# Another order of the parts of a steady step in a fused attention and feed-forward kernel

## The chip, the cores and the metric

The kernel runs on one core of a Trainium2 chip. The core has five engines that work side by side, each with its own queue of instructions in a fixed order: TensorE (PE in the profile; its weight loads are the row PEld), VectorE (DVE), ScalarE (ACT), GpSimd (POOL) and SyncE (SP, which here only issues DMAs). An instruction starts when its engine has come to it and when what it waits for is done. The metric is the device time of one execution in microseconds (us).

## The reference, cut to what matters

```python
scores = q @ k.T / sqrt(64)                      # 4 batches, 8 heads, 768 positions, 64 wide
keep   = (key < n_sink) | (0 <= row - key < window)      # 4 sinks, window of 128
a      = softmax(where(keep, scores, -1e9))
x      = (a @ v)  -> rows of 8 * 64 = 512        # 3072 tokens
h      = x @ w_in                                # 512 -> 2048
g      = max(h, 0) + log1p(exp(-abs(h)))
out    = g @ w_out                               # 2048 -> 512
```

## The kernel before

The 3072 tokens are cut into 12 chunks of 256 (three chunks to a batch). The work is laid out in steps: step i is head i % 8 of chunk i // 8, and in one step every part of the pipeline does one unit of its own: attention for one head, and one eighth of the two dense layers of an earlier chunk. All engines run their instructions in the order in which the Python code emits them, so the order of the parts within a step is the order of each engine's queue. Steps 0 to 16 are a list written out by hand (`Ctx.START`), with the loading of the weights between; from step 17 on `_fast` runs the parts J, j, G, L and then the letters of `Ctx.STEADY`: its second string where i % 8 is 0 (called the switch step below, because there the first dense layer goes over to the next chunk), its first string in the seven others. A step later than the switch step is called step 1 of the chunk, and so on to step 7.

The letters, with the lines and the tile names that the profile shows:

- S `scores` of head i + 4: 4 matmuls into `s` (lines 230, 231). T `softmax` of the same head: DVE masks and reduces `s` (243, 249), ACT takes exponentials (250). N `normalise`: DVE `sm`, `rc` (256, 257), and POOL scales `a` (264).
- W `weights_t` of head i: 2 transposes into `t` (297), ACT copies to `th`, DVE makes the rest `tl`, POOL masks both into `pt` (4 selects, 308 and 311). V `values`: 3 to 4 matmuls into `x` (327, 333) that need `pt`. O `out`: ACT copies `xt`, DVE adds `xt` and `xf` (351, 352); after an odd head ACT makes `xh` and POOL `xl` (DVE after head 7).
- p `split` of head i + 5 (ACT `qkh`, DVE the rests `qkh` and `kl`), q `split_v` (ACT and POOL, `vv`, odd steps alone), k and K the sink columns (`sa`, `ts`, `sk`, each fourth step).
- U: one eighth of the first dense layer, 24 matmuls into `h` (459). F `softplus`: three passes on ACT (466 to 468) into `mt`. P `gate`: DVE adds (474), POOL rounds to `gh` (52). R `residue`: DVE `gl`, the rest of the eighth before. D and E: the two halves of the second dense layer, two eighths behind U, 6 matmuls each (496 to 498) that need `gh` and `gl`.
- J and j put the sink values `vs` of a new batch in place on POOL (lines 151, 152, 60, 159), heads 0 to 3 at the start of step 6 and heads 4 to 7 at the start of step 1; in the steady part this happens three times each, when a batch ends. A weight check on DVE (440) follows most even steps.

Every product is done in parts: high and low halves of each operand are multiplied apart and added in PSUM, which is why there are so many splits. `t` and `x` have one PSUM buffer each, `s` and `h` two.

Of the kernel before, what the change touches and what calls it, by code (L numbers as in the profile page):

```python
# [834 lines left out]
Ctx.WT = "PAAVVVVAVAAVAAAVAAAAAAAAAAAPAAAV"  # L835
Ctx.WH = "VAPAAVAAAAVPPAAAAVVAVAAAAAVAVAAA"
Ctx.WL = "PPPPPPPVPPVPPVPPVPVPPPPVVPVVPVPV"
Ctx.STEADY = ("kWRqpUKFSTDPNVOE", "kqWRpSDKTUFNPVEO")
Ctx.START = """
S0 G4 T0 w w S1 j4 T1 J0 w L8 w w S3 S2 N0 N1 T2 W0 L10 w N2 S4 T3 N3 a w T4 k0 a c K0 a S5 c W1 w w  # L840
d S6 V0 O0 l d V1 w c l T5 N4 W2 T6 d w a S7 c O1 W3 l N5 G6 N6 a T7 c V2 N7 a d S8 k4 a O2 W4 w T8
# [62 lines left out]
```

## Time and profile before

| | |
|---|---|
| median of 3 runs | 738.54 us (738.09 to 738.7) |
| the profiled execution | 735.03 us |
| its span, first to last instruction | 733.3 us |
| mean granted clock of TensorE | 0.987 |
| PE busy | 699.0 us, 95% |
| DVE, ACT, POOL busy | 567.5, 448.7, 429.0 us |

The steady steps run from about 120 us to the end of the span; an ordinary one takes 6.8 to 6.9 us. Start times in the rows are us from the first instruction of the profiled execution.

### The profile page before, as it was taken

What the parts mean: (1) busy time and instruction counts of PE and PEld (TensorE: products, weight loads), DVE (VectorE), ACT (ScalarE), POOL (GpSimd) and SP (SyncE); (2) the same over time, 40 slices, a digit from 0 to 9 for tenths busy, and PEclk for the clock granted to TensorE, in tenths of its full rate; (3) what the DMA queues carried; (4) which work ended last, traced back from release to release, by engine and by line L of the source; (5) the groups of instructions that cost most, each with busy time, mean ns of one, the idle gap of its engine ahead of it and who ended that gap; (6) DMA issues with size and microseconds to landing.
All of it is one profiled execution on the core that took longest, in us unless ns stands there. A gap on an engine that the chain in (4) does not pass through costs nothing.

```text
span 733.3 us, 13867 instructions
## 1 busy us (share of the span) xinstructions
PE 699.0 (95%) x4489; PEld 621.4 (85%) x4489; DVE 567.5 (77%) x1608; ACT 448.7 (61%) x1098; POOL 429.0 (59%) x773
## 2 busy tenths in 40 slices
PE   4788899999999999999999999999999999999996
PEld 3567688988999999888898999998898998998995
DVE  5899997887887887887987988888887887754331
ACT  3577865765666666765666765765666666644331
POOL 4866476675655765775765665666666576563110
PEclk9899999999999999999999999999999999999998
DMA  8877611411321321312222222221222222100001
GB/s 299 298 261 227 196 40 48 119 53 44 100 67 48 106 67 49 103 55 60 74 74 67 77 77 67 77 75 46 71 66 78 77 67 77 60 11 1 29 1 35
DMA packets 40876, 63.21 MB, mean 86 GB/s; under 512 B 4635, under 2 KB 22363, under 8 KB 40795
## 3 DMA queue, kind: packets, MB, share of 16 engines
q1 hardware_dynamic: 36042, 45.47, 21.4%
q10 hardware_dynamic: 4752, 16.77, 6.7%
q8 instruction: 38, 0.62, 0.4%
q14 instruction: 44, 0.35, 0.2%
HBM read 55.93 MB, written 6.29 MB: 85 GB/s over the span
## 4 chain that ended last, share of the span: by engine, by line
PE 80%; DVE 7%; ACT 5%; POOL 5%; issue 2%; DMA 1%; ACTq 0%; SPq 0%; POOLq 0%; DVEq 0%
PE h L459 33%; PE acc L496 10%; PE acc L498 10%; PE acc L497 10%; PE x L333 6%; PE t L297 2%; PE s L230 2%; PE s L231 2%; ACT a L250 2%; PE x L327 2%; PE s L227 1%; DVE wt L403 1%; ACT mt L467 1%; ACT mt L468 1%; POOL vs L159 1%
## 5 line engine op out<-in xcount | busy, mean ns | idle before, releaser
L459 PE MATMUL h<-xh,wi 128*128 128x256 f32 x1536 | 254.1, 288 | 0.0
L459 PEld LDWEIGHTS h<-xh,wi 128*128 128x128 f32 x1536 | 211.7, 192 | 1.3 <-issue 0.3
L52 POOL TENSOR_SCALAR gh<-mt 128x512 fp32r<-128x512 f32 x91 | 56.6, 622 | 169.4 <-DVE mt L474 164.3
L459 PE MATMUL h<-xl,wi 128*128 128x256 f32 x768 | 154.7, 283 | 0.0
L496 PE MATMUL acc<-wo,gh 128*128 128x512 f32 x384 | 152.3, 397 | 0.0
L498 PE MATMUL acc<-wo,gl 128*128 128x512 f32 x384 | 151.3, 394 | 0.8 <-DVE gl L56 0.8
L497 PE MATMUL acc<-wo,gh 128*128 128x512 f32 x384 | 151.1, 393 | 0.0
L474 DVE SCALAR_TENSOR_TENSOR mt<-h,mt 128x512 f32<-128x512 f32 x96 | 66.1, 689 | 73.0 <-ACT mt L468 63.9
L466 ACT ACTIVATE mt<-h 128x512 f32<-128x512 f32 x96 | 57.1, 595 | 102.6 <-PE h L459 102.1
L459 PEld LDWEIGHTS h<-xl,wi 128*128 128x128 f32 x768 | 119.8, 192 | 0.0
L250 ACT ACTIVATE a<-a,stats 128x136 f32<-128x136 f32 x192 | 76.1, 397 | 59.7 <-DVE stats L249 59.7
L264 POOL TENSOR_SCALAR a<-a,rc 128x128 f32<-128x128 f32 x180 | 68.1, 390 | 43.0 <-ACT mt L466 28.3
L498 PEld LDWEIGHTS acc<-wo,gl 128*128 128x128 f32 x384 | 72.4, 189 | 17.7 <-DVE gl L56 1.2
L496 PEld LDWEIGHTS acc<-wo,gh 128*128 128x128 f32 x384 | 72.4, 189 | 13.0 <-issue 0.5
L56 DVE TENSOR_TENSOR gl<-mt,gh 128x512 fp32r<-128x512 f32 x96 | 77.4, 806 | 4.1 <-POOL gh L52 4.0
L497 PEld LDWEIGHTS acc<-wo,gh 128*128 128x128 f32 x384 | 72.5, 189 | 8.9
L308 POOL TENSOR_SCALAR_AFFINE_SELECT pt<-tl 128x256 fp32r<-128x256 f32 x80 | 57.9, 724 | 17.6 <-DVE tl L56 17.6
L467 ACT ACTIVATE mt<-mt 128x512 f32<-128x512 f32 x96 | 60.8, 633 | 3.1
L468 ACT ACTIVATE mt<-mt 128x512 f32<-128x512 f32 x96 | 60.7, 632 | 3.1
L48 ACT CAST qkh<-qk 128x656 fp32r<-128x656 f32 x80 | 59.5, 744 | 2.4 <-DMA qk<-qk 2.3
L308 POOL TENSOR_SCALAR_AFFINE_SELECT pt<-th 128x256 fp32r<-128x256 f32 (+1 forms) x96 | 41.8, 435 | 27.5 <-ACT th L48 20.2
L56 DVE TENSOR_TENSOR kl<-qk,qkh 128x400 fp32r<-128x400 f32 x80 | 53.7, 671 | 2.5
(183 smaller groups left out, 1247.2 us busy)
## 6 DMA issues: line engine op xcount, KB each, us to landing
qk<-qk SPq DMA_DIRECT2D x160, 164.0 KB, 3.0
vr<-v SPq DMA_DIRECT2D x32, 192.0 KB, 2.8
out<-o SPq DMA_DIRECT2D x24, 256.0 KB, 2.3
q<-q SPq DMA_DIRECT2D x8, 256.0 KB, 4.9
vr<-v SPq DMA_DIRECT2D x16, 128.0 KB, 2.2
k<-k SPq DMA_DIRECT2D x8, 200.0 KB, 4.8
wi00r<-w ACTq DMA_DIRECT2D x1, 511.8 KB
wi01r<-w ACTq DMA_DIRECT2D x1, 511.8 KB
```

Of the source, the lines that this page charges most:

```text
L48: nc.scalar.copy(out, in_)
L56: (nc.vector if eng == "V" else nc.gpsimd).tensor_tensor(out, a, b, ALU.subtract)
L250: nc.scalar.activation(a, a, AF.Exp, bias=nm, scale=-1.0, accum_out=sm[:, j : j + 1])
L264: (nc.vector if eng == "V" else nc.gpsimd).tensor_scalar(a, a, rc[:, j : j + 1], 0.0, ALU.mult, ALU.add)
L308: nc.gpsimd.affine_select(pt[:, e, :, 1], src[:], [[0, CH], [1, P]], ALU.is_ge, 0.0, base=0, channel_multiplier=-1)
L459: nc.tensor.matmul(h[:, j], wt, x, start=k == 0, stop=k >= len(prods) - 2, skip_group_check=True)
L467: nc.scalar.activation(t[:], t[:], AF.Exp, scale=-1.0)
L468: nc.scalar.activation(t[:], t[:], AF.Ln, bias=1.0)
L474: nc.vector.scalar_tensor_tensor(t[:], h[:], 0.0, t[:], ALU.max, ALU.add)
L496: nc.tensor.matmul(acc[:], gh[:, j, q], wh, start=f == 0, stop=False, skip_group_check=True)
L497: nc.tensor.matmul(acc[:], gh[:, j, q], wl, start=False, stop=False, skip_group_check=True)
L498: nc.tensor.matmul(acc[:], gl[:, j, q], wh, start=False, stop=f == 2 * FP - 1, skip_group_check=True)
```

## The change

One line: the two strings that give the order of the parts of a step from step 17 on.

```diff
-Ctx.STEADY = ("kWRqpUKFSTDPNVOE", "kqWRpSDKTUFNPVEO")
+Ctx.STEADY = ("kWUqpKSFTRDVPONE", "SWTkpUKERDNFPqVO")
```

No instruction is added or removed. What moves on each engine:

TensorE. In the seven other steps its order stays as it was (W, U, K, S, D, V, E). In the switch step it changes. The rows are from the switch step into chunk 8, `t_0` the transposes of head 0, `s_4` the scores of head 4, `acc` the second dense layer, `ts` the sink transposes, `h_0` the first dense layer. Before:

```order
L297 MATMUL t_0_7077<-ident,a_0_6730 128x128 x2
L230 MATMUL s_4_0_7096<-qkh_4_6993 128x264
L231 MATMUL s_4_0_7096<-kl_4_6996,qkh_4_6993 128x264
L230 MATMUL s_4_1_7099<-qkh_4_6993 128x264
L231 MATMUL s_4_1_7099<-kl_4_6996,qkh_4_6993 128x264
L496 MATMUL acc_0_6534<-wo_1193,gh_6_6949 128x512
L497 MATMUL acc_0_6534<-wo_1193,gh_6_6949 128x512
L498 MATMUL acc_0_6534<-wo_1193,gl_6_6988 128x512
L496 MATMUL acc_1_6535<-wo_1193,gh_6_6949 128x512
L497 MATMUL acc_1_6535<-wo_1193,gh_6_6949 128x512
L498 MATMUL acc_1_6535<-wo_1193,gl_6_6988 128x512
L281 MATMUL ts_0_7108<-ident,sa_0_7075 32x128 x2
```

And in the changed kernel, at the same place:

```order
L230 MATMUL s_4_0_7075<-qkh_4_7016 128x264
L231 MATMUL s_4_0_7075<-kl_4_7019,qkh_4_7016 128x264
L230 MATMUL s_4_1_7078<-qkh_4_7016 128x264
L231 MATMUL s_4_1_7078<-kl_4_7019,qkh_4_7016 128x264
L297 MATMUL t_0_7081<-ident,a_0_6728 128x128 x2
L459 MATMUL h_0_7109<-xh_6356,wi_316 128x256 x4
L459 MATMUL h_0_7109<-xl_6357,wi_316 128x256 x2
L459 MATMUL h_0_7109<-xh_6356,wi_316 128x256 x4
L459 MATMUL h_0_7109<-xl_6357,wi_316 128x256 x2
L459 MATMUL h_0_7109<-xh_6356,wi_329 128x256 x4
L459 MATMUL h_0_7109<-xl_6357,wi_329 128x256 x2
```

The 24 matmuls of U have moved ahead of the six of D; behind them now come K, E, D and, last, V (before: V, then E).

VectorE. In the seven other steps `gl` goes from ahead of the split to behind T, and `sm` and `rc` go behind `xt` and `xf`. In the switch step, from `tl_0` on, before:

```order
L56 TENSOR_TENSOR tl_0_7082<-t_0_7077,th_0_7080 128x256
L56 TENSOR_TENSOR gl_7_7089<-mt_7_7023,gh_7_7047 128x512
L56 TENSOR_TENSOR qkh_5_7091<-qk_5_6973,qkh_5_7091 64x256
L56 TENSOR_TENSOR kl_5_7094<-qk_5_6973,qkh_5_7091 128x400
L56 TENSOR_TENSOR sk<-ts_0_7108,sk 32x256
L243 COPY_PREDICATED s_4_0_7096<-diag,s_4_0_7096 128x128
L243 COPY_PREDICATED s_4_1_7099<-diag,s_4_1_7099 128x128
L249 ISA a_1_7113,stats<-s_4_0_7096,mask_141 128x136
```

And now:

```order
L56 TENSOR_TENSOR tl_0_7086<-t_0_7081,th_0_7084 128x256
L243 COPY_PREDICATED s_4_0_7075<-diag,s_4_0_7075 128x128
L243 COPY_PREDICATED s_4_1_7078<-diag,s_4_1_7078 128x128
L249 ISA a_1_7093,stats<-s_4_0_7075,mask_141 128x136
L249 ISA stats 128x1
L249 ISA a_1_7093,stats<-s_4_1_7078,mask_142 128x136
L249 ISA stats 128x1
L269 TENSOR_TENSOR sa_0_7102<-a_0_6728,rc_0_6729 128x64
L56 TENSOR_TENSOR qkh_5_7104<-qk_5_6973,qkh_5_7104 64x256
L56 TENSOR_TENSOR kl_5_7107<-qk_5_6973,qkh_5_7104 128x400
L56 TENSOR_TENSOR sk<-ts_0_7134,sk 32x256
L56 TENSOR_TENSOR gl_7_7145<-mt_7_7027,gh_7_7052 128x512
```

T stands first now, and `gl` last. On ACT the exponentials of T go ahead of `qkh` in the same way.

GpSimd. After an odd head `xl` goes ahead of the two scalings of N. The rows are the end of a step 5 and the start of the step 6 behind it, where J puts sink values in place (`vsh` to the second `vs`). Before:

```order
L52 TENSOR_SCALAR gh_5_4427<-mt_5_4403 128x512
L264 TENSOR_SCALAR a_0_4313<-a_0_4313,rc_0_4314 128x128 x2
L56 TENSOR_TENSOR xl_3940<-xf_4_4340,xh_3939 128x256
L151 TENSOR_SCALAR vsh_4452<-vsr_4450 64x128
L152 TENSOR_TENSOR vsr_4450<-vsr_4450,vsh_4452 64x128
L60 TENSOR_SCALAR vs_0_4455<-sk 64x512
L159 TENSOR_TENSOR vs_0_4455<-vsh_4452,hmask 64x4x64
```

And now:

```order
L52 TENSOR_SCALAR gh_5_4432<-mt_5_4407 128x512
L56 TENSOR_TENSOR xl_3940<-xf_4_4336,xh_3939 128x256
L264 TENSOR_SCALAR a_0_4311<-a_0_4311,rc_0_4312 128x128 x2
L151 TENSOR_SCALAR vsh_4452<-vsr_4450 64x128
L152 TENSOR_TENSOR vsr_4450<-vsr_4450,vsh_4452 64x128
L60 TENSOR_SCALAR vs_0_4455<-sk 64x512
L159 TENSOR_TENSOR vs_0_4455<-vsh_4452,hmask 64x4x64
```

The scalings stand between `xl` and whatever comes next on this engine.

## Rows read from the trace of the kernel before

**Rows 1.** Part 1 of the page: busy us, share of the span, instructions.
```profile
PE 699.0 (95%) x4489; PEld 621.4 (85%) x4489; DVE 567.5 (77%) x1608; ACT 448.7 (61%) x1098; POOL 429.0 (59%) x773
```
**Rows 2.** Waits of PE alone: waiter, releaser, us in total, times, longest.
```profile
PE x L333 <- POOL pt L311: 7.9, 7, 1.9
```
**Rows 3.** Single steps as windows: us, then busy time (count) of each engine, clock, DMA.
```profile
177.16:184.91 7.75, 7.09 (x47) 6.21 (x46) 7.08 (x16) 4.87 (x12) 5.42 (x10) 1.00 0.01 2
...
317.41:324.34 6.93, 6.93 (x47) 6.34 (x46) 6.18 (x19) 4.44 (x11) 4.96 (x10) 1.00 0.09 25
324.34:332.78 8.44, 7.21 (x47) 6.32 (x46) 6.40 (x16) 4.43 (x11) 7.08 (x15) 1.00 0.27 77
...
375.14:381.94 6.80, 6.80 (x46) 6.21 (x45) 6.14 (x18) 4.34 (x11) 4.48 (x10) 1.00 0.14 35
402.74:409.87 7.13, 7.13 (x47) 6.32 (x46) 6.18 (x17) 5.23 (x14) 4.18 (x7) 1.00 0.00 0
...
516.26:524.40 8.14, 7.08 (x46) 6.20 (x45) 7.31 (x19) 5.31 (x13) 5.93 (x11) 1.00 0.00 0
```
**Rows 4.** Timeline of PE in a switch step: start us, us, instructions.
```profile
339.71 0.38 PE L297 MATMUL t<-ident,a 128*128 128x128 f32 x2
339.85 0.37 PE L230 MATMUL s<-qkh 128*128 128x264 f32 x1
...
340.41 0.40 PE L496 MATMUL acc<-wo,gh 128*128 128x512 f32 x1
...
341.95 0.71 PE L459 MATMUL h<-xh,wi 128*128 128x256 f32 x4
...
344.89 0.28 PE L327 MATMUL x<-sk,vs 128*128 128x256 f32 x1
```
**Rows 5.** Timeline, POOL and PE, where J stands ahead of step 6.
```profile
324.11 0.72 POOL L264 TENSOR_SCALAR a<-a,rc 128x128 f32<-128x128 f32 x2
325.23 0.74 POOL L56 TENSOR_TENSOR xl<-xf,xh 128x256 fp32r<-128x256 f32 x1 [0.40 <-ACT xh L48]
...
327.95 0.81 POOL L159 TENSOR_TENSOR vs<-vsh,hmask 64x256 fp32r<-64x256 f32 x1
328.72 0.61 POOL L159 TENSOR_TENSOR vs<-vsr,hmask 64x256 fp32r<-64x256 f32 x1
329.29 0.40 POOL L308 TENSOR_SCALAR_AFFINE_SELECT pt<-th 128x256 fp32r<-128x256 f32 x1
...
330.82 0.74 PE L333 MATMUL x<-pt,vv 128*128 128x256 f32 x3 [1.23 <-POOL pt L311]
```
**Rows 6.** Chain that ended last, a switch step and the step 1 behind it: start us, us, what.
```profile
340.55 0.42 DVE xl L56
...
341.36 0.82 DVE gl L56
...
343.36 0.41 DVE sk L56
...
344.55 0.89 ACT a L250 x4
...
347.28 0.70 DVE mt L474
...
349.47 0.86 POOL vs L159 x2
```
**Rows 7.** Timeline, POOL and PE, in the step 2 that starts at 409.87.
```profile
413.23 0.86 POOL L308 TENSOR_SCALAR_AFFINE_SELECT pt<-tl 128x256 fp32r<-128x256 f32 x1
414.05 0.59 POOL L311 TENSOR_SCALAR_AFFINE_SELECT pt<-tl 128x256 fp32r<-128x256 f32 x1
...
414.95 0.63 PE L333 MATMUL x<-pt,vv 128*128 128x256 f32 x3
```
**Rows 8.** The same two in an ordinary step 6, which starts at 437.81.
```profile
441.11 0.74 POOL L311 TENSOR_SCALAR_AFFINE_SELECT pt<-tl 128x256 fp32r<-128x256 f32 x1
...
442.89 0.63 PE L333 MATMUL x<-pt,vv 128*128 128x256 f32 x3
```

## The prediction

> **What bounds the kernel now.** I read the page's first part first: PE is busy for 95% of the span, no other engine for more than 77% [rows 1]. Busy is not the same as never held up, so next came the waits of PE alone. After the start-up, one wait is left on that list: the values (V, line 333) wait for POOL's last select of `pt`, 7.9 us in seven waits [rows 2]. Then the steady part step by step. An ordinary step takes 6.93 us, or 6.80 in a first chunk of a batch, where V has one matmul less (the steps at 317.41 and 375.14) [rows 3], and PE has no gap in it. So the steady part is PE's own work plus the steps that are longer than that, of which there are three kinds:
>
> - step 6 with J ahead of it: 8.44 us at 324.34, 1.51 too long [rows 3], three times, 4.5 us;
> - step 1 of a batch's first chunk, with j ahead of it: 7.75, 7.72 and 8.14 (the first and the last of them stand in the rows) [rows 3], so 0.95 + 0.92 + 1.34 = 3.2 us;
> - step 1 of the other chunks: 7.13 at the one shown, 0.20 too long [rows 3]; the five that are long differ by no more than 0.13, 0.8 us together.
>
> In all 8.5 us. That is all that an order of the other engines can win; what it can lose has no such limit. A reader should see that the change leaves PE's order alone in seven steps of eight, so that its effect there must come through the time at which `pt` is ready.
>
> **The switch step and step 1.** PE's row shows the pieces: W starts at 339.71, S at 339.85, D at 340.41, U at 341.95, V at 344.89 [rows 4]. With S and W alone ahead of it, U starts 0.56 + 0.14 = 0.70 us into the step, not 2.24: 1.54 earlier. Does U then wait for `xh` and `xl` of head 7? Only its last quarter reads them, at about 0.70 + 0.75 x 2.94 = 2.9 us; `xl` was done at 340.97, 1.26 us into the step [rows 6]. No wait: cost nothing, with 1.6 us of cover. V goes from ahead of E to the end of the step; the `x` that it makes is read by ACT and DVE, and there DVE's `mt` stands ahead anyhow, which ran at 7.57 us into the step [rows 6], later than V's new end at about 7.0. That costs nothing either unless `mt` comes much earlier.
>
> On DVE, what stood between `tl` and T, from `gl` at 341.36 to the end of `sk` at 343.77, 2.4 us, no longer delays T [rows 6]. T held the exponentials on ACT, these held F, F held `mt`: the chain goes through just these rows. So T, the exponentials and, with U 1.54 earlier, F all come sooner. The gain does not reach `mt` whole: the split waits for ACT's `qkh`, now behind the exponentials, and `gl` (0.82) and the reciprocals stand right ahead of `mt`. Bounds: `mt` 0 to 1.54 us earlier. Laying the durations of that step end to end in the new order I get `mt` at 6.9 instead of 7.57, and take 0.65.
>
> Everything behind `mt` moves with it: `gh`, j's work, the selects, `tl` of step 1. In the three steps with j the first select came behind j's last row (349.47 and 0.86) [rows 6]; 0.65 earlier wins 0.65 of each wait at least, and more because `gl`, which ran beside these selects, is now behind T. Between 2.0 (3 x 0.65) and 3.2, I take **2.7**. In the five others 0.65 is more than the 0.1 to 0.2 that is lost: **0.8**. If `mt` comes no earlier, both are nothing.
>
> **The seven other steps.** DVE does `gl` behind T instead of ahead of the split. D needs it a step later, so more than 3 us cover it; the hole that it fills is the one in which DVE waited for F. `xt` and `xf` wait for ACT's `xt` copy, behind F and the exponentials, so they come as before. `sm` and `rc` now run in the hole in which DVE waits for the next `th`. Nothing here reaches PE; cost taken as nothing, covered by PE's 6.93 us step.
>
> POOL is different. After an odd head it did N's two scalings (0.72 us) while it waited 0.40 for ACT's `xh`, and then `xl` [rows 5]. Now `xl` cannot start sooner, since `xh` sets it, and the scalings come behind it, ahead of the next step's selects: these start up to 0.72 later. In an ordinary even step V started 442.89 - 441.85 = 1.04 us after the last select ended [rows 8], so 0.3 is left and the cost is nothing. In step 2 it was 414.95 - 414.64 = 0.31 [rows 7]; there the shift would cost up to 0.41, eight times 3.3 us, if nothing else moved. But step 2 was tight because DVE was late in step 1; with `mt` 0.65 earlier, `xh`, `xl` and `th` come as much earlier, and I take nothing.
>
> In step 6 with J there is no slack. `xl` ended at 325.97, J's work ran to 329.29, the selects followed, V waited [rows 5]. The scalings go straight in between: 0.72 later. Part of it comes back, since J's work also ran longer than it must (the two placings took 0.81 and 0.61 for the same size [rows 5]; the slow one ran beside the split on DVE). Bounds per step: 0.3 (0.72 less 0.4 for relief on the three rows that were slow) and 1.2 (0.72 plus 0.46, one select held as in rows 7, 0.86 against 0.40 alone in rows 5). I take 0.6, three times: **1.8** lost.
>
> What hits one select beside DVE is seen in rows 5 and 7: 0.40 alone, 0.86 beside `gl`. The Trainium skill (SBUF — State Buffer, section on the two separate sides) has a rule that speaks against this change: VectorE with two SBUF inputs and GpSimd take one port pair in turn, and the loser waits for the whole instruction. By it the sinks' work, pushed towards the place where `gl` now stands, would be held by `gl` in each of the three steps; that is the second rival. The rows agree in size, but do not show J's work beside `gl` in that place.
>
> **Sum.** -2.7 - 0.8 + 1.8 = -1.7 us. The profiled execution took 735.03 us, so 733.3. The median of the runs shown is 738.54, 3.5 us above it, and I give the prediction against the median: **736.8 us**. Its own range, with the bounds of the three terms, runs from -3.1 (-3.2 - 0.8 + 0.9) to -0.4 (-2.0 - 0.8 + 2.4): 735.4 to 738.1. About 0.2%, 1.5 us, is what a measurement can tell from no change, so this forecast itself lies partly within it.
>
> **Rivals.**
> 1. More of it: J's work gets all the relief (0.3 each) and the steps 1 lose all their waits, with the scalings partly hidden in `xl`'s old wait: -3.2 - 0.8 + 0.9 = -3.1, 735.4 us. For it: DVE has nothing to do between the split and T there.
> 2. J hit twice: the sinks' work is pushed beside `gl` and held by it, 1.2 each: -3.5 + 3.6 = 0.1, 738.6 us, no difference. For it: rows 7; against it: DVE is free for part of that time.
> 3. The order on the other engines does not matter, because the same work on POOL ends last in all these steps: 738.5 us. Against it: the three kinds of long steps all have a queue order ahead of the wait.
> 4. Slower: the switch step does not catch up. T waits for `tl`, and `tl` for the reciprocals behind `xl`; then `qkh`, `kl`, `sk` and `gl` pile up ahead of `mt`. If `mt` comes no earlier than 7.5 us into the step, step 1 stays as long as it is, step 2 stays tight, and the scalings cost 0.41 in each of eight: 0 + 3.3 + 1.8 = +5.1, 743.6 us. The point that decides is `mt`'s start in the switch step: 7.57 now, 6.9 forecast. Against it: 2.4 us of DVE's work leaves the way of T.
>
> **Numbers.** Chances: the forecast 0.55, rival 1 0.10, rival 2 0.17, rival 3 0.06, rival 4 0.12. Two thirds of the forecast's cases and rival 1 are faster by over 0.2%: 0.47. The rest of it and rivals 2 and 3 lie within: 0.41. Slower 0.12. For the range I leave rival 4 out and take the other cases with some 0.4 us of what the shown runs differ by: 735.0 to 739.0.
>
> **What would show it.** In the changed profile: `mt` of the switch step at about 6.9 us in it; step 1 at 6.80 to 6.95 where it was 7.0 to 7.2, and under 7.2 with j; step 6 with J at 8.7 to 9.6; ordinary steps unchanged at 6.93 and 6.80; the wait of V for POOL at about 6 us instead of 7.9. A wait of U for `xh`, or of V in step 2, would break the sum; so would `gl` arriving late at D.

## The result, and the profile after

The changed kernel takes 739.13 us (median of 21 runs), the kernel before 737.85 in as many runs beside it: the ratio is 1.0025, with a 95% interval of 1.0014 to 1.0036. It is slower by a quarter of a per cent, where 736.8 us and a gain were forecast. The profiled execution has a span of 735.7 us against 733.3, 2.4 us more.

Part 1 of the page after, which answers to [rows 1]:

```profile
PE 699.7 (95%) x4489; PEld 624.8 (85%) x4489; DVE 552.6 (75%) x1608; ACT 446.1 (61%) x1098; POOL 400.7 (54%) x773
```

PE has the same instructions and, to within 0.7 us, the same busy time; DVE and POOL are even less busy than before, by 15 and 28 us with the same instructions. That did not help. PE's waits after, beside [rows 2] (7.9 us in seven waits):

```profile
PE x L333 <- POOL pt L311: 9.8, 6, 2.4
```

Both lists hold one wait of 1.9 us that lies in the start-up, ahead of the steps that the change touches. Of the others, the three in step 6 with J went from 1.23 to 2.38 us each, the three in step 1 of the first chunks (0.64 to 1.06) are gone, and two of 0.4 in step 2 of a first chunk are new. Single steps after, as windows with the columns of [rows 3] (us, busy time of the engines, then the granted clock); the line in the second fence is the step 2 of a first chunk before:

```profile
155.04:162.68 7.64, 5.25 (x39) 4.71 (x37) 4.45 (x14) 4.06 (x10) 6.49 (x13) 0.98 0.29 84
162.68:166.07 3.39, 3.39 (x9) 2.72 (x10) 1.67 (x6) 0.37 (x1) 0.95 (x3) 0.53 0.02 5
...
180.03:186.84 6.81, 6.81 (x47) 6.22 (x46) 6.23 (x15) 3.88 (x9) 4.77 (x11) 1.00 0.11 32
186.84:194.33 7.49, 7.10 (x47) 6.22 (x46) 6.75 (x19) 5.87 (x17) 4.04 (x9) 1.00 0.48 144
326.60:336.21 9.61, 7.22 (x48) 6.32 (x47) 5.22 (x17) 4.44 (x11) 7.02 (x13) 1.00 0.23 65
...
405.91:412.84 6.93, 6.93 (x48) 6.34 (x47) 6.32 (x18) 4.81 (x12) 4.36 (x9) 1.00 0.11 34
```
```profile
184.91:191.74 6.83, 6.83 (x47) 6.21 (x46) 5.68 (x17) 5.20 (x14) 4.07 (x9) 1.00 0.49 149
```

Read against [rows 3]: step 1 of a first chunk is 6.81 us instead of 7.75, step 1 of another chunk 6.93 instead of 7.13; both gains are there in full. But step 6 with J takes 9.61 us instead of 8.44, and the first of the three (the two windows from 155.04) 11.03 in all, of which the last 3.39 us ran at a granted clock of 0.53. And the step 2 behind a first chunk's step 1, 6.83 us before, takes 7.49 here and in one other of the three first chunks.

The 78 intervals between the transposes of one step and those of the next, from step 17 on, can be summed by kind. Each number is the difference to the kernel before in us, from one profiled execution each (step 7 and the switch step are taken together, since the transposes moved within the latter). "First" are the chunks that begin a batch, with the steps 6 and 7 ahead of them.

| kind (number) | before | whole change | e1 | e2 | e3 | e4 | e5 | e6 | e7 | e8 |
|---|---|---|---|---|---|---|---|---|---|---|
| step 6 with J (3) | 25.32 | +4.92 | +0.91 | +0.03 | +5.48 | +4.75 | -4.52 | -4.52 | -4.51 | +4.88 |
| step 1, first (3) | 23.61 | -3.18 | -3.19 | -2.15 | -0.10 | +0.58 | -3.18 | -3.18 | -3.19 | -2.18 |
| step 2, first (3) | 20.50 | +1.31 | +1.28 | -0.07 | -0.04 | +1.30 | -0.01 | -0.01 | +0.22 | -0.05 |
| step 1, others (7) | 49.35 | -0.81 | -0.81 | -0.77 | -0.35 | -0.34 | -0.82 | -0.81 | +0.01 | -0.77 |
| step 2, others (7) | 48.60 | +0.02 | +0.02 | +0.02 | -0.04 | +4.15 | +0.03 | +0.02 | -0.04 | +1.67 |
| step 7 and switch (18) | 126.13 | -0.11 | -0.10 | -0.09 | +2.56 | +1.48 | -0.13 | -0.13 | +0.06 | -0.11 |
| all other steps | 255.82 | +0.05 | +0.05 | +0.06 | +0.10 | -0.12 | +0.03 | +0.04 | +0.02 | -0.10 |
| sum | 549.33 | +2.20 | -1.84 | -2.97 | +7.61 | +11.80 | -8.60 | -8.59 | -7.43 | +3.34 |

The sum of the whole change, +2.2, accounts for nearly all of the 2.4 us of span. Four of its rows make it up, the first four; the experiments take them one by one.

### The profile page after: what moved, and what is told of

Same layout as the page of the kernel before. It is cut to its first block, busy times and chain, and to the rows that moved or that the text cites. A ratio compares the mean times of both kernels' runs of the same rounds, so it can differ in the third digit from the quotient of the medians.

```text
span 735.7 us, 13883 instructions
## 1 busy us (share of the span) xinstructions
PE 699.7 (95%) x4489; PEld 624.8 (85%) x4489; DVE 552.6 (75%) x1608; ACT 446.1 (61%) x1098; POOL 400.7 (54%) x773
## 4 chain that ended last, share of the span: by engine, by line
PE 83%; DVE 6%; POOL 4%; ACT 3%; DMA 1%; issue 1%; ACTq 0%; SPq 0%; POOLq 0%; DVEq 0%
PE h L459 34%; PE acc L496 11%; PE acc L498 11%; PE acc L497 11%; PE x L333 6%; PE t L297 2%; PE s L230 2%; PE s L231 2%; PE x L327 2%; PE s L227 1%; ACT a L250 1%; POOL a L264 1%; DMA wo71r<-w 1%; POOL pt L308 1%; PE ts L281 1%
## 5 line engine op out<-in xcount | busy, mean ns | idle before, releaser
L264 POOL TENSOR_SCALAR a<-a,rc 128x128 f32<-128x128 f32 x180 | 71.9, 411 | 87.1 <-DVE rc L257 78.8
L56 DVE TENSOR_TENSOR gl<-mt,gh 128x512 fp32r<-128x512 f32 x96 | 70.5, 734 | 4.4 <-POOL gh L52 4.0
L351 DVE TENSOR_TENSOR xt<-x,xt 64x256 f32<-64x256 f32 x80 | 33.2, 415 | 38.9 <-ACT xt L48 38.9
L243 DVE COPY_PREDICATED s<-diag,s 128x128 f32<-128x128 int32 x192 | 49.1, 289 | 15.4 <-PE s L231 11.9
L333 PE MATMUL x<-pt,vv 128*128 128x256 f32 (+1 forms) x216 | 48.7, 328 | 7.9 <-POOL pt L311 7.9
```

The costliest lines, as they stand in the source:

```text
L56: (nc.vector if eng == "V" else nc.gpsimd).tensor_tensor(out, a, b, ALU.subtract)
L264: (nc.vector if eng == "V" else nc.gpsimd).tensor_scalar(a, a, rc[:, j : j + 1], 0.0, ALU.mult, ALU.add)
L333: nc.tensor.matmul(x[:, :, o], w, pt[:, :, m], start=False, stop=n == 2, skip_group_check=True)
```

## The experiments

Theory A: the scalings of N, now behind `xl`, push the sink work of J, and with it the selects and the values of step 6. Theory B: `gl` in its new place, or the new switch step, holds the sink work. Theory C: the steps 1 were won by `gl`'s new place, not by the switch step.

**e1: N ahead of O again.**

```diff
-Ctx.STEADY = ("kWUqpKSFTRDVPONE", "SWTkpUKERDNFPqVO")
+Ctx.STEADY = ("kWUqpKSFTRDVPNOE", "SWTkpUKERDNFPqVO")
```

> The changed order with one pair of letters put back: N ahead of O in the seven other steps, so POOL does the two scalings before xl again. Theory A (the scalings behind xl push the sink work of J, and so the values in step 6): step 6 with J falls from 9.6 us to 8.4 or less, no stretch of lower TensorE clock is left behind it, step 2 of a batch's first chunk falls from 7.49 to about 6.9, and the steps 1 keep what they won: about 4 us under the kernel before, ratio 0.994 to 0.996. Theory B (gl behind T, or the new switch step, holds the sink work): step 6 with J stays over 9 us and the ratio stays at 1.000 to 1.003.

Measured: ratio 0.9978 (0.9962 to 0.9994), 2.2 permille faster than the kernel before instead of 2.5 slower. The windows of e1, a step 6 with J and the step 2 of a first chunk:

```profile
323.96:332.72 8.76, 7.22 (x48) 6.33 (x47) 6.09 (x17) 4.44 (x11) 7.39 (x15) 1.00 0.24 67
184.41:191.67 7.26, 7.10 (x46) 6.20 (x45) 6.28 (x19) 5.84 (x17) 3.95 (x8) 1.00 0.42 129
```

One pair of letters turns the result round: step 6 falls from 9.61 to 8.76, and the stretch at a lower clock is gone. So theory A holds for the larger part. It does not hold for all: 8.76 is not 8.44, and step 2 stays at 7.26. Both remainders must come from the parts that e1 shares with the change, and so 2 us of the forecast 4 are missing. For step 6 it is `gl` in its new place. POOL's first select there and DVE's `gl` beside it:

```profile
328.72 0.89 POOL L308 TENSOR_SCALAR_AFFINE_SELECT pt<-th 128x256 fp32r<-128x256 f32 x1
```
```profile
328.38 0.97 DVE L56 TENSOR_TENSOR gl<-mt,gh 128x512 fp32r<-128x512 f32 x1
```

The select took 0.40 in the same place before [rows 5].

**e2 and e3: the change cut in two**, the new switch step with the old seven others (e2, the first line), and the other way round (e3).

```diff
+Ctx.STEADY = ("kWRqpUKFSTDPNVOE", "SWTkpUKERDNFPqVO")
```
```diff
+Ctx.STEADY = ("kWUqpKSFTRDVPONE", "kqWRpSDKTUFNPVEO")
```

> The new order in the switch step alone, the old one in the seven others. Theory A: the steps 1 are shortened here too, since it is the switch step that brings mt forward (6.81 with j instead of 7.7 to 8.1, 6.93 instead of 7.0 to 7.15), step 6 with J stays at 8.44: 3 to 4 us faster, ratio 0.995 to 0.996. Theory C (the steps 1 were won by gl behind T in the other steps): the steps 1 stay as before, no more than 1 us won.

> The new order in the seven other steps alone, the old switch step. Theory A: step 6 with J at 9.6 us (+1.2 each, 3.5 in all), the steps 1 long as before or a little less, and step 2, whose selects now stand behind the scalings, up to 0.4 us longer in eight places: 4 to 8 us slower than before, ratio 1.005 to 1.011. Theory C: the steps 1 are short, the ratio is that of the whole change, 1.002 to 1.004.

Measured: e2 0.9956 (0.9939 to 0.9973), e3 1.0083 (1.0063 to 1.0102). Most of the good is in the switch step, all the harm in the order of the seven others. In e2 step 6 with J is as long as before (8.45 us). In e3 the steps 1 gain almost nothing (-0.10 and -0.35), which refutes theory C taken alone. But with e2 the steps 1 of first chunks give 2.15 us, not the 3.18 of the whole change: `gl` behind T adds a third of that gain once the switch step is new (e8, below, puts it back and has 2.18).

One part of what e3 was expected to do did not come. Its steps 2, where the scalings stand ahead of the selects, were to be up to 0.4 us longer in eight places; they are as long as before (-0.04 in both rows of the table). A step 2 of e3, and `mt` in its switch step, which starts at 346.38:

```profile
300.34:307.28 6.94, 6.94 (x47) 6.33 (x46) 6.00 (x19) 4.92 (x12) 4.56 (x9) 1.00 0.56 162
```
```profile
354.28 0.69 DVE L474 SCALAR_TENSOR_TENSOR mt<-h,mt 128x512 f32<-128x512 f32 x1 [1.44 <-ACT mt L468]
```

`mt` comes 7.90 us into the step, later than before, so it is not an earlier `mt` that spares step 2 here.

**e4: N behind O in the kernel before, nothing else.**

```diff
-Ctx.STEADY = ("kWRqpUKFSTDPNVOE", "kqWRpSDKTUFNPVEO")
+Ctx.STEADY = ("kWRqpUKFSTDPVONE", "kqWRpSDKTUFNPVEO")
```

> The kernel before with N moved behind O in the seven other steps and nothing else. Theory A: step 6 with J goes from 8.44 to 9.2 to 9.6 us, and step 2 from 6.95 to up to 7.35, since nothing brings xh forward there; the rest unchanged: 2.5 to 7 us slower, ratio 1.003 to 1.009. Theory B: step 6 with J stays within 0.3 us of 8.44, ratio 1.000 to 1.002.

Measured: 1.0158 (1.0136 to 1.0180), 11.8 us in the table where 2.5 to 7 were expected. Windows of e4, a step 2 and a step 6 with J, and PE's row of V in that step 2:

```profile
302.03:309.66 7.63, 7.23 (x47) 6.33 (x46) 6.09 (x18) 5.37 (x13) 5.08 (x9) 1.00 0.54 165
330.66:341.59 10.93, 8.58 (x47) 7.42 (x46) 6.05 (x20) 4.43 (x11) 7.35 (x15) 0.84 0.19 62
```
```profile
307.70 0.73 PE L333 MATMUL x<-pt,vv 128*128 128x256 f32 x3 [0.40 <-POOL pt L311]
```

The 0.40 is the price that the fourth rival of the prediction gave for step 2, and the step is longer by more than that, 7.63 against 6.95. In the kernel before, step 2 has no room for the scalings. `gl` behind T is enough to make it: e3, with `gl` there and the old switch step, loses nothing. The new switch step alone is not quite enough: e8, below, with that and `gl` ahead of the split, still has five of these steps at 7.13 (a sixth, at 7.65, follows a switch step from the hand-written list). POOL's first select in these steps 2, in e4 and then in e3, shows why:

```profile
305.20 0.85 POOL L308 TENSOR_SCALAR_AFFINE_SELECT pt<-th 128x256 fp32r<-128x256 f32 x1
```
```profile
303.17 0.41 POOL L308 TENSOR_SCALAR_AFFINE_SELECT pt<-th 128x256 fp32r<-128x256 f32 x1
```

In e4 it runs beside `gl` (DVE, from 305.04 to 305.78), in e3 `gl` comes two microseconds later. The 10.93 holds a stretch at a lower clock (mean 0.84), which I had not expected either.

**e8: `gl` ahead of the split again, the rest of the change kept.**

```diff
-Ctx.STEADY = ("kWUqpKSFTRDVPONE", "SWTkpUKERDNFPqVO")
+Ctx.STEADY = ("kWRUqpKSFTDVPONE", "SWTkpUKERDNFPqVO")
```

> The whole change with one letter put back: R ahead of the split in the seven other steps, so gl is where it was, while the scalings stay behind xl. Theory A (the scalings): the wait of the values in step 6 with J stays at about 2.35 us. Theory B (gl behind T holds the sink work): it falls to 1.3 to 1.6 us. If the long step 2 of two first chunks comes from gl's place too, it falls from 7.49 to 6.85.

Timed once, so without an interval: 738.22 us. The row of V in a step 6 with J, and POOL's scalings in the same step:

```profile
333.07 1.22 PE L333 MATMUL x<-pt,vv 128*128 128x256 f32 x3 [2.37 <-POOL pt L311]
```
```profile
327.07 1.42 POOL L264 TENSOR_SCALAR a<-a,rc 128x128 f32<-128x128 f32 x2
```

The wait stays at 2.37 us: theory B is refuted where N stands behind O. The waits of V in step 6 now make a square: N first and `gl` early 1.23 (before) and 1.24 (e2); N first and `gl` late 1.54 (e1); N late and `gl` early 2.35 (e4) and 2.38 (e8); N late and `gl` late 2.39 (the change and e3). N costs 0.85 to 1.1, `gl` 0.3 if N is first and nothing if N is late: in its old place it lies beside the late scalings, which take 1.42 us here instead of 0.72 [rows 5]. Step 2 of first chunks is 6.8 us here (-0.05 for the three), as against 7.49: in the whole change that loss is `gl`'s. It needs the new switch step too, since e3 does not have it (-0.04); in e4, with the old switch step and `gl` ahead, the late scalings bring as much (+1.30).

**e5, e6, e7: the sink work behind the selects.** J and j go behind W, in e2's order (e5, the second diff), in that of the whole change (e6, the third), and in that of before (e7, the last); the first diff is in all three.

```diff
-            for part in "JjGL" + c.STEADY[i % H == 0]:
+            for part in "GL" + c.STEADY[i % H == 0]:
```
```diff
+Ctx.STEADY = ("kWJjRqpUKFSTDPNVOE", "SWTkpUKERDNFPqVO")
```
```diff
+Ctx.STEADY = ("kWJjUqpKSFTRDVPONE", "SWTkpUKERDNFPqVO")
```
```diff
+Ctx.STEADY = ("kWJjRqpUKFSTDPNVOE", "kqWRpSDKTUFNPVEO")
```

> The new order in the switch step alone (as in the second experiment), and the sink work J and j moved from the start of its step to behind W, so that POOL does it after the selects of that step. Theory A (the values wait because the sink work stands ahead of the selects): step 6 with J and step 1 with j fall to ordinary length, 6.93 and 6.80 us; with the 3.0 us of the second experiment, some 4.5 us of J and 1.1 us of j, about 8.5 us under the kernel before: ratio 0.987 to 0.991. Rival: the same work delays gh, the scalings and the next step's selects, and the wait only moves to steps 7 and 2: ratio 0.993 to 0.997.

> The whole change, with J and j behind W. Theory A: the scalings behind xl cost only where the sink work follows them ahead of the selects; with that gone, step 6 with J falls from 9.6 to 6.93, no stretch of lower TensorE clock is left in the steady part, and steps 1 keep their gain: 7 to 8.5 us under the kernel before, ratio 0.989 to 0.991. Rival: the scalings hold the selects in the other even steps too, and no more than 4 us is won.

> The kernel before with J and j behind W and nothing else. Theory A: the 4.5 us of the three steps 6 and the 3.2 us of the three steps 1 with j go, the 0.8 us of the other steps 1 stays: 7 to 7.7 us faster, ratio 0.989 to 0.991. Rival as in the fifth experiment: the wait moves to the next step, 2 to 4 us faster.

Measured: e5 0.9867 (0.9847 to 0.9887), e6 0.9864 (0.9843 to 0.9885), e7 0.9880 (0.9864 to 0.9896); e6 and e7 gain more than the 0.989 to 0.991 expected of them. The timeline of POOL in e6, where the changed order stands with J behind W:

```profile
322.99 0.74 POOL L56 TENSOR_TENSOR xl<-xf,xh 128x256 fp32r<-128x256 f32 x1 [1.08 <-ACT xh L48]
323.71 0.94 POOL L264 TENSOR_SCALAR a<-a,rc 128x128 f32<-128x128 f32 x2
...
326.01 0.40 POOL L311 TENSOR_SCALAR_AFFINE_SELECT pt<-tl 128x256 fp32r<-128x256 f32 x1
326.39 0.29 POOL L151 TENSOR_SCALAR vsh<-vsr 64x128 fp32r<-64x128 f32 x1
```

The scalings still stand behind `xl` and still take 0.94, but the selects come next and are done at 326.41, and V waits for nothing: PE's waits for `pt` in e6 are the one of 1.9 us in the start-up. The 8.5 us that the prediction counted as all that an order can win are won, to within 0.1 (-8.60 and -8.59). The rivals, that the wait moves to the next step, are refuted by the rows of steps 7 and 2. And e5 and e6 are equal: with the sink work out of the way, the order that made the kernel slower does no harm at all. By the medians e5, e6 and e7 gain 0.8 to 1.7 us more than the table shows; 0.8 to 0.9 us of their shorter spans lie behind the last matmul, and what shortened that is not shown.

## Why the prediction was wrong

**What bounds the kernel: right.** PE's work plus three kinds of long steps, 8.5 us, all behind `pt`. e5 and e6 won just that in these steps. One reading was off, without bearing on the sum: of the 7.9 us of [rows 2], 1.9 are the wait in the start-up.

**The switch step and step 1: right, and sized too low.** Rows after, PE's S at the start of the switch step and DVE's `mt`:

```profile
343.14 0.28 PE L230 MATMUL s<-qkh 128*128 128x264 f32 x1
```
```profile
349.61 0.67 DVE L474 SCALAR_TENSOR_TENSOR mt<-h,mt 128x512 f32<-128x512 f32 x1
```

`mt` starts 6.47 us into the step, forecast 6.9, before 7.57 [rows 6]. The two terms were -2.7 and -0.8; they measured -3.2 and -0.8. Of the 3.2, the switch step alone gives 2.15 (e2), and the rest comes with `gl` out of the way of the selects, as the prediction had it: the first select of such a step takes 0.90 us in e2, beside `gl`, and 0.40 in the change. Rival 4, by which the switch step does not catch up, fell at its own point.

**The failed step: the scalings ahead of J, +0.6 a step.** It measured 9.61 - 8.44 = 1.17, near the upper bound of 1.2, three times 3.5 us instead of 1.8. Two rows of POOL before, that stand between those of [rows 5]:

```profile
325.95 0.29 POOL L151 TENSOR_SCALAR vsh<-vsr 64x128 fp32r<-64x128 f32 x1
326.32 0.77 POOL L152 TENSOR_TENSOR vsr<-vsr,vsh 64x128 f32<-64x128 f32 x1
```

Rows of POOL after, which answer to them and to [rows 5]:

```profile
328.22 0.93 POOL L264 TENSOR_SCALAR a<-a,rc 128x128 f32<-128x128 f32 x2
329.12 0.60 POOL L151 TENSOR_SCALAR vsh<-vsr 64x128 fp32r<-64x128 f32 x1
329.80 0.45 POOL L152 TENSOR_TENSOR vsr<-vsr,vsh 64x128 f32<-64x128 f32 x1
...
331.04 1.13 POOL L159 TENSOR_TENSOR vs<-vsh,hmask 64x256 fp32r<-64x256 f32 x1
332.14 0.60 POOL L159 TENSOR_TENSOR vs<-vsr,hmask 64x256 fp32r<-64x256 f32 x1
```

and of DVE beside them:

```profile
328.48 0.42 DVE L56 TENSOR_TENSOR qkh<-qk,qkh 64x256 fp32r<-64x256 f32 x1
328.93 0.63 DVE L56 TENSOR_TENSOR kl<-qk,qkh 128x400 fp32r<-128x400 f32 x1
...
331.02 0.69 DVE L56 TENSOR_TENSOR gl<-mt,gh 128x512 fp32r<-128x512 f32 x1
```

The relief that I counted on came almost only for one row (`vsr`, 0.45 instead of 0.77), but the scalings took 0.93 instead of 0.72 beside the split, `vsh` 0.60 instead of 0.29 beside `kl`, and the first placing 1.13 instead of 0.81: it starts 0.02 behind `gl` and ends 0.46 after it. That is the second rival's mechanism, to the place. The three losses, 0.21, 0.31 and 0.32, outweigh the relief: of the 1.17, 0.72 are the scalings' own time, and some 0.45 is what the neighbours added. The Trainium skill (SBUF — State Buffer, section on the two separate sides) has it that of a VectorE instruction with two SBUF inputs and a GpSimd instruction that reads SBUF the later one waits until the other is done. The trace agrees as far as it goes: the placing outlasts `gl`, by 0.46 us, which is less than the 0.60 that the second placing takes alone. But the square shows that `gl` is not needed in that place for a wait of 2.38: with `gl` ahead of the split (e8, e4) the wait is the same, since there it is the scalings that lie beside it. The work moved past one collision meets another.

**What was not in the sum: a lower clock around the end of the long wait.** The first of the three steps lost 1.4 us more (11.03 against 9.61). PE after:

```profile
162.68 1.22 PE L333 MATMUL x<-pt,vv 128*128 128x256 f32 x3 [2.38 <-POOL pt L311]
163.69 0.63 PE L496 MATMUL acc<-wo,gh 128*128 128x512 f32 x1
```

Behind the wait of 2.38 us V's three matmuls took 1.22 instead of 0.73, and the six of E started 0.43 apart instead of 0.23; the granted clock over this stretch was 0.53, the lower of its two levels, 1.2 GHz, for nearly all of it. So this wait cost more than its length; the two others of the change, as long as it, did not. The loss is not the profiled execution's alone: the mean granted clock of the 21 timed executions of the change is 0.986 in the median, that of the 30 executions of the kernel before beside the experiments 0.988. 3.5 + 1.4 is the +4.9 of the table.

**The other steps: one was missed.** "Nothing here reaches PE" failed in the step 2 of two first chunks, +1.3 us. Rows of the step 1 ahead of one, DVE and POOL:

```profile
353.19 2.19 DVE L56 TENSOR_TENSOR qkh<-qk,qkh 64x256 fp32r<-64x256 f32 x1
```
```profile
353.12 0.40 POOL L308 TENSOR_SCALAR_AFFINE_SELECT pt<-th 128x256 fp32r<-128x256 f32 x1
353.48 0.29 POOL L311 TENSOR_SCALAR_AFFINE_SELECT pt<-th 128x128 fp32r<-128x128 f32 x1
353.73 0.40 POOL L308 TENSOR_SCALAR_AFFINE_SELECT pt<-tl 128x256 fp32r<-128x256 f32 x1
354.09 0.29 POOL L311 TENSOR_SCALAR_AFFINE_SELECT pt<-tl 128x128 fp32r<-128x128 f32 x1
354.36 0.74 POOL L56 TENSOR_TENSOR vv<-vr,vv 128x256 fp32r<-128x256 f32 x1
```

With `gl` gone from ahead of it, the split's `qkh` comes just behind POOL's first select and takes 2.19 us instead of 0.42: it ends 0.28 after the last of five POOL instructions that follow each other without a gap. So `kl`, T, `gl` and `mt` are late, `xh` with them, and the next step's V. e1 has such a `qkh` in all three first chunks and the long step 2 with it; e8, with `gl` ahead of the split, has neither. (e6 has one of 1.96 us in three steps 7, which are no longer for it.) The cover that I had named, DVE's 0.65 us of lead, went here. I had priced a POOL instruction held by DVE, not DVE held by POOL.

For the other steps 2 the price of nothing came true, but not for the reason given. The prediction had `mt` 0.65 us earlier pay for the scalings there; by e8, that alone would have left 0.18 us in five steps. It is `gl`'s new place that pays in full, with `mt` later than before in e3, so that term was right in part by luck, and the 3.3 us that rival 4 put on step 2 do not come in e3, where `mt` is as late as that rival has it. By the difference of the whole change and e8, `gl`'s move won 1.0 us in the steps 1 and 1.65 in the other steps 2, and lost 1.36 in the step 2 of the first chunks.

**Sum.** Forecast -2.7 - 0.8 + 1.8 = -1.7; measured -3.2 - 0.8 + 3.5 + 1.4 + 1.3 = +2.2. The gains were better than forecast; the loss of the queue that I had seen was twice its estimate, and two losses were not seen.

Left open: what decides whether a wait of 2.4 us costs clock; why the `qkh` of the third first chunk got in behind the first select (0.72 us, started 0.04 behind it) where the two others (0.05 and 0.07 behind theirs) waited for all five; and why step 7 and the switch step are 1.5 us longer in e3 and e4 (the other 1.1 us of e3's 2.6 are a lower clock that reaches into one of its steps 7, of 8.03 us). The experiments did not go into these.

## What to carry to other kernels

Where one engine is the bound and all its waits end on another's queue, look in that queue for work that is not urgent and stands ahead of what is: putting it behind (e7, two letters) won 1.2%, and made the two orders of the other parts equally fast (e5, e6). Price a move by what it puts ahead of the urgent instructions at the tightest step, at the duration that it has beside its new neighbours; a share of relief that is not read from a row is hope. Judge halves of a reordering apart: here one half was worth -0.4% and the other +0.8%.

## What the runs showed of the hardware

The granted clock fell to its lower level around the end of a wait of 2.35 to 2.39 us, or up to 1.5 us behind it, in 5 of the 12 steps 6 that had one (one of three in the change, in e4 and in e8, two in e3), and cost 1.4 to 1.5 us each time; at nine waits of 1.23 to 1.54 us (before, e1, e2) it never did in the profiled executions. What decides between the twelve was not tried. And a VectorE subtraction with two inputs from SBUF took 2.19 us instead of 0.42 when it started 0.07 us behind the first of five GpSimd instructions without a gap, and ended after the last of them, while in the rows shown GpSimd's placing was held by `gl` alone and for no longer than `gl` ran.
